# Three instead of two groups of the down product by seven products, with part of their weights narrowed earlier

## The chip, the core and the metric

The kernel runs on one core of a Trainium2 chip. The metric is the time of one execution in device microseconds (us); lower is better. The engines are TensorE (PE, matmuls; PEld is its weight load), VectorE (DVE), ScalarE (ACT), GpSimd (POOL) and SyncE (SP), which only issues DMAs here. Each engine works off its own list of instructions in order and waits on semaphores of the others.

## The reference

```python
# q, k, v: (4, 12, 448, 64)
scores = scale * np.matmul(q, k.transpose(0, 1, 3, 2))
scores = np.einsum('bhij,hg->bgij', scores, w_pre)
attn = softmax(scores)                       # over the last axis
attn = np.einsum('bhij,hg->bgij', attn, w_post)
x = np.matmul(attn, v)                       # heads put side by side: (4, 448, 768)
h = x.transpose(0, 2, 1) @ U @ V             # rank 32
u = x + h.transpose(0, 2, 1)
out = u + np.maximum(u @ w_ch1, 0.0) @ w_ch2 # 768 -> 3072 -> 768
```

An attention whose scores are mixed across the 12 heads before and after the softmax, and then a two-layer feed-forward part. The weights and U, V come as float64, so each is brought to float32 on the chip.

## The kernel before

**Stages.** The attention goes through 17 units of query rows, cut into 180 chunks; two chunks make one step. A step is a premix (matmuls with w_pre, line 502), a negated row maximum on DVE (L509), two exponents on ACT (L514), a small chain over POOL (L517), DVE (L520) and POOL (L524) that scales w_post, a postmix (56 matmuls, L538) and a copy out of PSUM (L346 on ACT, L348 on DVE). Scores (L441) are relayed by DMA on SP into a second layout (L462), and the product with v is L579 and L587. Then the rank-32 part, and from about 371 us the up product (L1056) and the down product (L1159 and L1333).

**Float32 from two parts.** For the feed-forward matmuls each operand is split into a high part and a low part, and a product is three matmuls. A split is a high half (a copy, L346 on ACT or L350 on POOL) and a low half (a subtraction, L353 on DVE or POOL), for weight tiles `w` (384 columns) and hidden tiles `u` (448 columns).

**Narrowing.** A piece of weights (128 x 384) arrives as pairs of words in a tile `kr` (DMA, L706). Five steps make float32 of it: the absolute value (L718 on ACT or L720 on DVE), then on DVE L724 with L725, L729, and L733 with L734, and a last addition L738 on POOL or DVE. The result goes to a tile `aw`, or to the single tile `ea`; from `ea` it is stored in DRAM and loaded again into `aw` when it is due (`put` and `take`: L996 and L999 for w1, L1226 and L1229 for w2). The eight pieces of the first two groups of w1 go that way during the attention.

**The down product.** w2 has 24 blocks of 128 rows. In a plain group of n rows ("S4": four rows), every batch and column block is a sum of 3n matmuls (L1159), gathered two blocks at a time by DVE (L1162); the hidden tiles are made by ACT (L1141) and DVE (L1145). In a group by seven products ("W": four rows), two batches and two column halves are computed together by seven products of mixed operands: weights are mixed at L884, hidden tiles at L1288, both on DVE or POOL, and split (L353); a block is 7 x 6 matmuls (L1333), with one copy between banks on ACT (L346) and six accumulations on DVE (L1356). Before the change four plain groups come first and two groups by seven products last; the sixteen weight pieces of the latter are narrowed through `ea` during the down product.

**What sets the order.** A planner (`Plan.order`) goes through all steps with an assumed duration for each and writes one list per engine. Ready steps are taken by rank, the smallest first; the ranks are built from the numbers in `RANK`. In the attention one unit of rank is one chunk. Steps that may run on two engines go where the planner sees the earlier end. Rings limit how far ahead it can work: 9 tiles `aw`, 21 split weight tiles, 21 split hidden tiles, 10 tiles `hs` of hidden rows, one `ea`, two `kr`, four PSUM banks of two halves.

The piece's rank and gate before the change:

```python
re = D0 + RANK["wp0"] + i * RANK["wps"]
narrow(key, src, HW, 128, re, "open_tail", partial(early_tile, key), [("ea", key)])
```

`D0` is the rank at which the down product begins, `NC` = 180 that at which the attention ends, and "open_tail" a point after the attention.

Of the kernel before, what the change touches and what calls it, by code (L numbers as in the profile page):

```python
# [34 lines left out]
HW = DM // 2  # L35
# [9 lines left out]
class Unit:  # L45
# [10 lines left out]


RANK = dict(
    e0=-99.572, estep=11.251, er=3.851, qk_lead=4.489, qk_step=0.807, av_off=3.434, av_step=1.544, post=4.6,
    kr=0.972, vr=0.941, qr=3.511, mx=1.793, ex=0.535, ep=1.385, po=3.438, qo=1.291, uv0=7.458, uvs=-0.011,  # L60
    uv1=1.407, raw=4.445, k0=-12.657, kstep=1.04, m0=8.907, pu=1.842, ev=14.526, lead=17.128, t0=-3.523,
    ts=0.611, t1=2.276, ta=38.195, tb=2.957, dl=28.391, hl=9.338, out=3, wp0=0.291, wps=18.345, wf=10.916,
    hw=8.471, hq=2.597, w1=3.04, w2=1.082, st=-3.0, un=6.124, w3=1.324,
)


GROUPS = ["S4"] * 4 + ["W"] * 2


CAPS = dict(qk=2, pre=3, post=3, av=2, lr=2, aq=2, bb=2, dn=3)  # L70
# [26 lines left out]
def words(ap):  # L97
    return ap.bitcast(I32).rearrange("p (n t) -> p n t", t=2)
# [165 lines left out]
def build(tc, q2, kt, vj, wpre_in, wpost_in, u_in, v_in, ident, w1j, w2, out, show=None):  # L264
# [64 lines left out]
    def uses(key, *at, first=False):  # L329
        for ring, k in at:  # L330
            users.setdefault((ring, k), []).append(key)
            if first:
                makers[ring, k] = key
# [57 lines left out]
    NC = len(chunks)  # L391
# [73 lines left out]
    for u, un in enumerate(units):  # L465
        b, size = un.b, 128 * (H // 2) * un.cols
        src = q2[at:at + size].rearrange("(p h i) -> p h i", p=128, h=H // 2)
# [80 lines left out]
    for k in range(NC // 2):  # L548
        r = 2 * k
        us = sorted({chunks[2 * k][0], chunks[2 * k + 1][0]})  # L550
        pre, post, st, e, wr = ("pre", k), ("post", k), ("st", k), ("e", k), ("wr", k)
        ts = [("t", u) for u in us]
# [204 lines left out]
    def early():  # L757
        c = NC + RANK["e0"] + n_early[0] * RANK["estep"]
        n_early[0] += 1
        return ("premix", max(0, int(c) // 2)), c + RANK["er"]  # L760
# [102 lines left out]
    def when(F, p, j):  # L863
        return U0 + PU * (7 * nth[F, p] + POS[j])
# [32 lines left out]
    for p in range(2):  # L897
        b0, b1 = 2 * p, 2 * p + 1
        gates = [[None] + ["open_qk"] * 3 + ["open_t1"] * 2 + ["open_mix"], ["open_tail", "open_x1", "open_x0", "open_uv", "open_uv", "open_x2", "open_x3"]][p]
        for i in range(3):  # L900
# [13 lines left out]
            t3, t2, t4, t1 = (("T", p, j, i) for j in (1, 2, 4, 5))  # L914
# [13 lines left out]
            key = ("again", i)  # L928
# [49 lines left out]
    for F in range(NF):  # L978
        r = [when(F, 0, j) - RANK["lead"] for j in range(7)]
        pieces = ((A11, 0, 0, 0), (A21, 1, 0, 1), (A22, 1, 1, 2), (A12, 0, 1, 3))  # L980
        gate = "open_qk" if F == 0 else "open_tail"
        done = {}
        for i, f, h, j in pieces:
            key = ("w", F, i)
            src = words(w1j[2 * F + f][:, h * HW:(h + 1) * HW])
# [4 lines left out]
            g, re = early()  # L990
# [84 lines left out]
    for n, (F, p) in enumerate(chains):  # L1075
# [8 lines left out]
        ev = [when(F, p, j) - RANK["ev"] for j in range(7)]  # L1084
# [13 lines left out]
    D0 = U0 + PU * 7 * NU  # L1098
    after("open_end", open_end, [("P", NU - 1, j) for j in range(7)])

    groups, base, f0, t = [], [], 0, D0
    for kind in GROUPS:
        n = 4 if kind == "W" else int(kind[1:])
# [7 lines left out]
    def take_up(ring, n=1):  # L1111
        at = [(ring, count[ring] + i) for i in range(n)]
        count[ring] += n
        return at
# [15 lines left out]
    def aw_at(k):  # L1130
        return lambda: at[pick(*k)]
# [85 lines left out]
    def early_piece(key, src, r):  # L1217
        i = pieces_w[0]
        pieces_w[0] += 1
        re = D0 + RANK["wp0"] + i * RANK["wps"]  # L1220
        narrow(key, src, HW, 128, re, "open_tail", partial(early_tile, key), [("ea", key)])
        kd = take_up("aw")[0]

        def put(eng):
            T["nf", key] = dram.tile([128, HW], F32, "nf" + "_".join(str(k) for k in key))
            eng.dma_start(out=T["nf", key], in_=T["na", key])  # L1226

        def take(eng):
            eng.dma_start(out=aw_at(kd)(), in_=T["nf", key])  # L1229

        plan.add((key, "put"), [("SP", (480, 900))], put, re, [(key, 4)], [("ea", key)])
        plan.add((key, "take"), [("SP", (480, 900))], take, r - RANK["raw"], [(key, "put")])
        uses((key, "take"), kd, first=True)
        return kd, (key, "take")
# [213 lines left out]
```

## Time and profile before

| | us |
|---|---|
| median of 3 runs | 1030.43 (1028.73 to 1030.83) |
| profiled execution | 1032.64 |
| its span, first to last instruction | 1030.8 |
| PE busy in the span | 987.8 (96%) |
| DVE busy | 787.6 (76%) |
| ACT busy | 501.1 (49%) |
| POOL busy | 362.9 (35%) |

The profile is of one execution. Busy shares are means over stages with different limits, so what a change is worth is read from its own stage. Matmuls are pipelined: a single one of 448 columns is listed with 363 ns, and its pace is read from how many end in a stretch. The idle time in front of an instruction is put down to what came last before it.

### The profile page before, as it was taken

Reading aid. Unit: us, or ns where it says so; the run is one execution under the profiler, and the core shown is the slowest. Engines: PE = TensorE matmul, PEld = TensorE weight load, DVE = VectorE, ACT = ScalarE, POOL = GpSimd, SP = SyncE. Lnnn points to the kernel's source line nnn. Section 1 sums busy time; section 2 is a strip of 40 time slices with the busy share of each in tenths; the row PEclk is TensorE's granted clock in tenths of the full one; section 3 lists DMA queues with packets and bytes.
Section 4 is the critical chain, followed back from the end, with each engine's and each line's share of the span. In section 5 each row is a group of like instructions: output and inputs, shape, how many; then the busy total and the mean of one; then the engine's idle time right before and its main releaser. Section 6 shows DMA issues by size and latency. Waiting matters only on the chain. (4 is left out here: it accounts for less than half of the span.)

```text
span 1030.8 us, 29018 instructions
## 1 busy us (share of the span) xinstructions
PE 987.8 (96%) x11964; PEld 826.7 (80%) x11964; DVE 787.6 (76%) x1303; ACT 501.1 (49%) x1038; POOL 362.9 (35%) x469
## 2 busy tenths in 40 slices
PE   7889998999989899999999999999999999999998
PEld 2556665665656589899999999999999999998987
DVE  3375764676566868989998878894899999879985
ACT  4576776767867864543333333341232332435440
POOL 4021121213111554343523434220223236647670
PEclk9999999999999999999999999999999999999999
DMA  6665657576566536445455444687354553344143
GB/s 206 203 184 170 208 173 206 160 250 174 180 205 198 160 138 217 145 139 176 153 162 148 133 137 146 201 277 299 105 176 144 175 161 115 116 139 122 49 153 115
DMA packets 96267, 173.13 MB, mean 168 GB/s; under 512 B 11576, under 2 KB 77064, under 8 KB 96136
## 3 DMA queue, kind: packets, MB, share of 16 engines
q1 hardware_dynamic: 95716, 170.64, 52.7%
q8 instruction: 94, 1.54, 0.7%
q10 hardware_dynamic: 420, 0.65, 0.2%
q14 instruction: 37, 0.30, 0.1%
HBM read 92.04 MB, written 40.50 MB: 129 GB/s over the span
## 5 line engine op out<-in xcount | busy, mean ns | idle before, releaser
L1056 PE MATMUL bank<-u,w 128*128 128x448 f32 x1512 | 305.9, 363 | 2.3 <-DVE hs L1069 1.7
L1056 PEld LDWEIGHTS bank<-u,w 128*128 128x128 f32 x1512 | 283.7, 188 | 22.6 <-DVE hs L1069 1.6
L1159 PE MATMUL bank<-u,w 128*128 128x448 f32 x1152 | 230.7, 362 | 0.0
L1159 PEld LDWEIGHTS bank<-u,w 128*128 128x128 f32 x1152 | 216.0, 188 | 14.4
L738 POOL TENSOR_TENSOR aw<-aw,x 128x384 f32<-128x384 f32 x69 | 77.2, 1120 | 187.6 <-DVE x L734 184.0
L538 PEld LDWEIGHTS bank<-wr,e 60*64 60x64 f32 x5040 | 90.7, 135 | 46.9 <-issue 29.1
L509 DVE TENSOR_REDUCE st<-bank 128x2 f32<-128x896 f32 x90 | 96.8, 1085 | 40.4 <-PE bank L502 38.9
L514 ACT ACTIVATE e<-bank,st 128x448 f32<-128x448 f32 x180 | 112.7, 638 | 21.5 <-DVE st L509 13.9
L346 ACT CAST w<-aw 128x384 fp32r<-128x384 f32 x111 | 56.2, 514 | 129.8 <-POOL aw L738 49.7
L538 PE MATMUL bank<-wr,e 60*64 60x60 f32 x5040 | 94.9, 220 | 15.5 <-issue 7.7
L1333 PE MATMUL bank<-u,w 128*128 128x448 f32 x504 | 102.6, 363 | 3.6 <-ACT bank L346 2.5
L1333 PEld LDWEIGHTS bank<-u,w 128*128 128x128 f32 x504 | 94.0, 188 | 11.9 <-ACT bank L346 3.6
L441 PE MATMUL bank<-k,q 64*64 64x448 f32 (+1 forms) x768 | 92.4, 559 | 5.7 <-DMA k<-in_kt 1.9
L517 POOL TENSOR_SCALAR st<-st 128x2 f32<-128x2 f32 x90 | 19.9, 221 | 210.1 <-ACT e L514 204.5
L502 PE MATMUL bank<-t,wpre 64*64 64x448 f32 x720 | 86.3, 550 | 6.7 <-ACT e L514 2.4
L346 ACT COPY hs<-bank 128x448 f32<-128x448 f32 x90 | 47.8, 533 | 73.4 <-PE bank L1056 69.5
L346 ACT COPY a<-bank 128x840 f32<-128x840 f32 (+1 forms) x73 | 62.1, 853 | 37.4 <-PE bank L538 36.0
L353 POOL TENSOR_TENSOR w<-aw,w 128x384 fp32r<-128x384 f32 x59 | 67.2, 1142 | 35.2 <-ACT w L346 34.5
L579 PEld LDWEIGHTS bank<-a,v 128*64 128x64 f32 x1224 | 56.6, 137 | 21.6 <-ACT a L346 6.0
L1162 DVE TENSOR_TENSOR acc<-acc,bank 128x896 f32<-128x896 f32 x48 | 51.8, 1083 | 26.3 <-PE bank L1159 26.2
L734 DVE SCALAR_TENSOR_TENSOR x<-kr,x 128x384 f32<-128x384 uint32 (+2 forms) x99 | 64.8, 655 | 3.4
L579 PE MATMUL bank<-a,v 128*64 128x120 f32 (+4 forms) x1224 | 63.5, 258 | 4.0 <-ACT a L346 2.2
(81 smaller groups left out, 1267.7 us busy)
## 6 DMA issues: line engine op xcount, KB each, us to landing
hd<-hs SPq DMA_DIRECT2D x96, 224.0 KB
hs<-hd SPq DMA_DIRECT2D x96, 224.0 KB
t<-s SPq DMA_DIRECT2D x102, 210.0 KB
kr<-in_w1j SPq DMA_DIRECT2D x48, 384.0 KB
kr<-in_w SPq DMA_DIRECT2D x48, 384.0 KB
v<-in_vj SPq DMA_DIRECT2D x24, 256.0 KB
q<-in_q SPq DMA_DIRECT2D x30, 186.0 KB
ud<-acc SPq DMA_DIRECT2D x12, 448.0 KB
```

The costliest lines, as they stand in the source:

```text
L346: eng.copy(out=o, in_=i)
L353: eng.tensor_tensor(out=o, in0=a, in1=b, op=ALU.subtract)
L441: eng.matmul(o[at, i, :S], lhsT=q[d, pj, of], rhs=k[d, pj, :], start=True, stop=True)
L502: eng.matmul(o[64 * j:64 * j + 64, i, :S], lhsT=wpre[64 * i:min(64 * i + 64, QW)], rhs=tt[side(u)][64 * i:min(64 * i + 64, QW), n, :], sta ...
L509: eng.tensor_reduce(out=mx, in_=T["pre", k][:, :, :S], axis=AX.X, op=ALU.max, negate=True)
L514: eng.activation(out=e[:, i], in_=T["pre", k][:, i, :S], func=ACTF.Exp, bias=T["mx", k][:, i:i + 1], accum_out=sm[:, i:i + 1])
L538: eng.matmul(d, lhsT=e[64 * j:64 * j + HALF, i, x * KB:x * KB + KB], rhs=wr[64 * j:64 * j + HALF, i].rearrange("p (g m) -> p g m", m=MH), ...
L579: eng.matmul(main[i * D:(i + 1) * D, c, :n], lhsT=v[:, p + c, i, x, :], rhs=a[:, x * H + 2 * (p + c) + i, :n], start=(c == 0 and x == 0), ...
L738: eng.tensor_tensor(out=f32(a), in0=f32(a), in1=f32(x), op=ALU.add)
L1056: eng.matmul(o, lhsT=w[:, x, i * 128:(i + 1) * 128], rhs=u[:, i, y, :], start=j < 2 and i + t == 0, stop=i + t == 4, skip_group_check=True)
L1159: eng.matmul(ps[:, j, :S], lhsT=wd_tile(wk[i0][f])[:, x, cc * 128:(cc + 1) * 128], rhs=h_tile(hk[f])[:, y, :], start=(i == 0), stop=(i == ...
L1333: eng.matmul(o, lhsT=wd_tile(wk[j, F])[:, x, i * 128:(i + 1) * 128], rhs=h_tile(hk[j, F])[:, y, :], start=j < 2 and t == 0, stop=t == len( ...
```

## The change

The groups become three plain and three by seven products. The first fourteen of now twenty-four weight pieces of the latter are ranked into the attention, one each 9.6 chunks from chunk 30 on, each gated by a premix; the other ten stay in the down product. The planner's numbers are set anew, among them the step of the eight w1 pieces (from 11.3 to 13.0 chunks). Nothing else is changed, so the order of all engines differs in many places.

```diff
 RANK = dict(
-    e0=-99.572, estep=11.251, er=3.851, qk_lead=4.489, qk_step=0.807, av_off=3.434, av_step=1.544, post=4.6,
...
+    e0=-99.572, estep=13.022, er=3.667, qk_lead=4.144, qk_step=0.788, av_off=4.502, av_step=1.544, post=4.6,
...
+    hw=11.881, hq=2.597, w1=4.321, w2=1.082, st=-3.0, un=5.826, w3=1.281, we=-150, ws=9.631,
 )
-GROUPS = ["S4"] * 4 + ["W"] * 2
+GROUPS = ["S4"] * 3 + ["W"] * 3
+
+
+AHEAD = 14
@@
     def early_piece(key, src, r):
         i = pieces_w[0]
         pieces_w[0] += 1
-        re = D0 + RANK["wp0"] + i * RANK["wps"]
-        narrow(key, src, HW, 128, re, "open_tail", partial(early_tile, key), [("ea", key)])
+        re, gate = D0 + RANK["wp0"] + max(0, i - AHEAD) * RANK["wps"], "open_tail"
+        if i < AHEAD:
+            c = NC + RANK["we"] + i * RANK["ws"]
+            re, gate = c + RANK["er"], ("premix", min(max(0, int(c) // 2), NC // 2 - 1))
+        narrow(key, src, HW, 128, re, gate, partial(early_tile, key), [("ea", key)])
```

Line numbers up to the function above grow by 3, those behind it by 6. In the rows that follow, a tile's number tells one buffer from another.

DVE in the attention, between two row maxima some 32 steps in, before and after (`st` the row maxima and sums, `a` and `s` the copies out of PSUM, `t` and `u` parts of the rank-32 part and of the up product's operand):

```order
L348 COPY a_321<-bank_60 128x42x20
L520 RECIPROCAL st_271<-st_271 128x2
L509 TENSOR_REDUCE st_252<-bank_58 128x2
L520 RECIPROCAL st_433<-st_433 128x2
L353 TENSOR_TENSOR u<-acc,u 128x448
L520 RECIPROCAL st_252<-st_252 128x2
L601 TENSOR_TENSOR acc<-acc,bank_60 128x3x11x5
L509 TENSOR_REDUCE st_259<-bank_59 128x2
```

```order
L723 TENSOR_SCALAR x_791<-kr_690 128x384
L356 TENSOR_TENSOR t_0_1907<-bank_59,t_0_1907 32x256
L727 TENSOR_SCALAR x_791<-x_791 128x384
L728 TENSOR_SCALAR ea_790<-x_791 128x384
L732 SCALAR_TENSOR_TENSOR ea_790<-kr_690,ea_790 128x384
L833 TENSOR_TENSOR acc<-acc,bank_60 128x2x448
L736 TENSOR_SCALAR x_791<-ea_790 128x384
L737 SCALAR_TENSOR_TENSOR x_791<-kr_690,x_791 128x384
L512 TENSOR_REDUCE st_433<-bank_59 128x2
```

A whole narrowing (L723 to L737) now stands in front of a row maximum there.

PE at the end of the attention, before and after (`wr`, `e`: postmix; `a`, `v`: the product with v; `u`, `w`: the up product):

```order
L538 MATMUL bank_60<-wr_282,e_261 64x12x5 x24
L538 MATMUL bank_60<-wr_282,e_261 64x60 x4
L538 MATMUL bank_59<-wr_319,e_274 64x12x5 x24
L538 MATMUL bank_59<-wr_319,e_274 64x60 x4
L538 MATMUL bank_61<-wr_354,e_285 64x12x5 x24
L538 MATMUL bank_61<-wr_354,e_285 64x60 x4
L1045 MATMUL bank_58<-u,w_5539 128x448 x2
L1056 MATMUL bank_60<-u,w_5539 128x448 x9
L579 MATMUL bank_59<-a_321,v_267 64x100 x18
```

```order
L541 MATMUL bank_61<-wr_282,e_261 64x12x5 x24
L541 MATMUL bank_61<-wr_282,e_261 64x60 x4
L1048 MATMUL bank_60<-u,w_5644 128x448 x2
L1059 MATMUL bank_59<-u,w_5644 128x448 x9
L541 MATMUL bank_61<-wr_319,e_274 64x12x5 x24
L541 MATMUL bank_61<-wr_319,e_274 64x60 x4
L1059 MATMUL bank_59<-u,w_5645 128x448 x9
L541 MATMUL bank_58<-wr_354,e_285 64x12x5 x24
L541 MATMUL bank_58<-wr_354,e_285 64x60 x4
L582 MATMUL bank_61<-a_321,v_267 64x100 x18
```

Two products of the up product (L1059) moved between the last three postmixes.

DVE in the blocks by seven products, in the second group of each, before and after (`acc<-bank,acc`: accumulations; `u<-hs,u`: low halves of hidden tiles; `hs<-hs,hs`: mixings of hidden tiles; `ea`, `x`: narrowing):

```order
L1356 TENSOR_TENSOR acc<-bank_59,acc 128x448
L724 TENSOR_SCALAR x_930<-x_930 128x384
L725 TENSOR_SCALAR ea_790<-x_930 128x384
L353 TENSOR_TENSOR u<-hs_5956,u 128x448
L729 SCALAR_TENSOR_TENSOR ea_790<-kr_824,ea_790 128x384
L1356 TENSOR_TENSOR acc<-bank_58,acc 128x448 x2
L1356 TENSOR_TENSOR acc<-bank_59,acc 128x448
L733 TENSOR_SCALAR x_930<-ea_790 128x384
L734 SCALAR_TENSOR_TENSOR x_930<-kr_824,x_930 128x384
```

```order
L1294 TENSOR_TENSOR hs_6090<-hs_6090,hs_6088 128x448
L1362 TENSOR_TENSOR acc<-bank_59,acc 128x448 x2
L1362 TENSOR_TENSOR acc<-bank_60,acc 128x448
L356 TENSOR_TENSOR u<-hs_6090,u 128x448
L1294 TENSOR_TENSOR hs_6094<-hs_6089,hs_6091 128x448
L1362 TENSOR_TENSOR acc<-bank_61,acc 128x448
L1362 TENSOR_TENSOR acc<-bank_60,acc 128x448
L356 TENSOR_TENSOR u<-hs_6094,u 128x448
L1362 TENSOR_TENSOR acc<-bank_58,acc 128x448
L356 TENSOR_TENSOR u<-hs_6087,u 128x448
```

The narrowing is gone from this place, and mixings and low halves stand between the accumulations.

## Rows read from the trace of the kernel before

**Rows 1.** Windows by stage: stretch, busy us of each engine (instructions), clock, DMA.
```profile
57.70:360.80 303.10, 284.11 (x7310) 188.33 (x7304) 196.58 (x332) 222.50 (x483) 70.66 (x184) 0.99 0.61 189
...
690.00:920.50 230.50, 230.50 (x1154) 216.12 (x1153) 197.59 (x306) 68.56 (x131) 86.21 (x78) 1.00 0.50 161
920.50:1027.90 107.40, 103.06 (x508) 94.40 (x507) 88.06 (x129) 46.16 (x92) 58.19 (x48) 1.00 0.37 119
```

**Rows 2.** A window inside the sums, and the sums' matmuls: ns min/median/max, first and last.
```profile
700.00:750.00 50.00, 50.00 (x252) 46.88 (x251) 32.83 (x51) 10.78 (x21) 7.79 (x8) 1.00 0.55 196
...
L1159 PE MATMUL bank<-u,w x1152: 360/363/364, 688.1 to 920.1; 128*128 128x448 f32 x192
```

**Rows 3.** Timeline of PE in the blocks: start, us, instruction [idle before <-what ended it].
```profile
951.08 15.88 PE L1333 MATMUL bank<-u,w 128*128 128x448 f32 x78 [1.86 <-ACT bank L346]
967.36 27.95 PE L1333 MATMUL bank<-u,w 128*128 128x448 f32 x138 [0.39 <-DVE acc L1356]
```

**Rows 4.** Window from the first to the 55th accumulation, columns as in rows 1.
```profile
923.90:1001.20 77.30, 74.38 (x367) 68.24 (x367) 68.76 (x99) 41.53 (x83) 52.74 (x44) 1.00 0.37 114
```

**Rows 5.** DVE's groups by form in that window: count | busy, mean ns | idle before.
```profile
L1356 DVE TENSOR_TENSOR acc<-bank,acc 128x448 f32<-128x448 f32 x52 | 30.8, 616 | 9.1 <-PE bank L1333 5.9 <-ACT bank L346 3.0
L353 DVE TENSOR_TENSOR u<-hs,u 128x448 fp32r<-128x448 f32 x16 | 17.0, 1072 | 0.0
L1288 DVE TENSOR_TENSOR hs<-hs,hs 128x448 f32<-128x448 f32 x11 | 10.3, 957 | 0.0
L729 DVE SCALAR_TENSOR_TENSOR ea<-kr,ea 128x384 int32<-128x384 int32 x3 | 2.9, 967 | 0.0
...
L353 DVE TENSOR_TENSOR w<-aw,w 128x384 fp32r<-128x384 f32 x3 | 2.1, 694 | 0.0
L884 DVE TENSOR_TENSOR aw<-aw,aw 128x384 f32<-128x384 f32 x2 | 2.0, 990 | 0.0
...
L733 DVE TENSOR_SCALAR x<-ea 128x384 int32<-128x384 int32 x3 | 1.5, 506 | 0.0
```

**Rows 6.** DVE's narrowing and copies by form from 170 to 350 us.
```profile
L348 DVE COPY s<-bank 124x896 f32<-124x896 f32 x10 | 10.9, 1086 | 5.8 <-PE bank L441 5.0 <-issue 0.4 <-ACT e L514 0.2
...
L734 DVE SCALAR_TENSOR_TENSOR x<-kr,x 128x384 f32<-128x384 uint32 x8 | 4.7, 582 | 0.3
L729 DVE SCALAR_TENSOR_TENSOR ea<-kr,ea 128x384 int32<-128x384 int32 x8 | 4.4, 550 | 0.1
...
L725 DVE TENSOR_SCALAR ea<-x 128x384 int32<-128x384 int32 x8 | 3.0, 381 | 0.3
L724 DVE TENSOR_SCALAR x<-x 128x384 f32<-128x384 f32 x8 | 2.9, 362 | 0.1
L733 DVE TENSOR_SCALAR x<-ea 128x384 int32<-128x384 int32 x8 | 2.8, 352 | 0.1
L720 DVE TENSOR_SCALAR x<-kr 128x384 int32<-128x384 int32 x7 | 2.5, 358 | 3.6 <-DMA kr<-in_w1j 3.6
```

**Rows 7.** Three gaps of PE in the attention, from its timeline.
```profile
178.40 0.37 PE L538 MATMUL bank<-wr,e 60*64 60x60 f32 x3 [2.65 <-issue]
...
251.90 0.98 PE L502 MATMUL bank<-t,wpre 64*64 64x448 f32 x8 [0.99 <-DVE acc L601]
...
298.16 1.62 PE L579 MATMUL bank<-a,v 128*64 128x90 f32 x36 [1.47 <-ACT e L514]
```

**Rows 8.** The last postmix on PE.
```profile
369.15 1.45 PE L538 MATMUL bank<-wr,e 60*64 60x60 f32 x56 [1.84 <-ACT a L346]
```

**Rows 9.** DVE's low half of a hidden tile alone, and beside an instruction of POOL.
```profile
954.34 0.61 DVE L353 TENSOR_TENSOR u<-hs,u 128x448 fp32r<-128x448 f32 x1
...
960.98 1.16 POOL L353 TENSOR_TENSOR u<-hs,u 128x448 fp32r<-128x448 f32 x1 [3.80 <-ACT u L346]
...
963.19 1.27 POOL L1288 TENSOR_TENSOR hs<-hs,hs 128x448 f32<-128x448 f32 x1
...
963.37 1.57 DVE L353 TENSOR_TENSOR u<-hs,u 128x448 fp32r<-128x448 f32 x1
```

More of the change, by code (lines that the diff above doesn't have):

```diff
@@ L58 @@
 RANK = dict(
-    e0=-99.572, estep=11.251, er=3.851, qk_lead=4.489, qk_step=0.807, av_off=3.434, av_step=1.544, post=4.6,
[L60 to L63, printed above, removed]
-)
-GROUPS = ["S4"] * 4 + ["W"] * 2
+    e0=-99.572, estep=13.022, er=3.667, qk_lead=4.144, qk_step=0.788, av_off=4.502, av_step=1.544, post=4.6,
+    kr=0.972, vr=0.969, qr=3.511, mx=1.793, ex=0.535, ep=1.385, po=2.659, qo=1.291, uv0=7.458, uvs=0.277,
+    uv1=1.407, raw=3.874, k0=-11.774, kstep=1.03, m0=9.512, pu=1.661, ev=14.526, lead=17.128, t0=-3.523,
+    ts=1.27, t1=2.44, ta=38.195, tb=2.957, dl=31.544, hl=9.338, out=2.962, wp0=0.291, wps=17.853, wf=8.982,
+    hw=11.881, hq=2.597, w1=4.321, w2=1.082, st=-3.0, un=5.826, w3=1.281, we=-150, ws=9.631,
+)
+GROUPS = ["S4"] * 3 + ["W"] * 3
+AHEAD = 14
 CAPS = dict(qk=2, pre=3, post=3, av=2, lr=2, aq=2, bb=2, dn=3)
```

## The prediction

> **What bounds the kernel now.** I read the stretches first, then the gaps of TensorE (PE), then what the other engines do around them. From 690 us on, the down product runs: PE is busy 230.50 of 230.50 us in the plain sums, and 103.06 of 107.4 us in the two groups by seven products [rows 1]. In the sums 252 matmuls take 50.00 us [rows 2], so a matmul of 448 columns costs 0.1984 us and PE knows no wait there. VectorE (DVE) is nearly as full: 197.59 of 230.5 us in the sums and 88.06 of 107.4 us in the blocks [rows 1]. The attention is different: from 57.7 to 360.8 us PE has 284.11 us of work in 303.1 us, DVE 196.58, ScalarE (ACT) 222.50, GpSimd (POOL) 70.66 [rows 1]. There PE waits for short chains, and room is left on DVE. So fewer matmuls shorten the end one for one, as long as DVE and POOL can feed PE in the blocks and the attention does not pay for what is moved into it.
>
> **Part 1: one plain group becomes a group by seven products.** A plain group of four rows of w2 has 4 batches x 6 blocks x 4 rows x 3 = 288 matmuls; by seven products it has 2 x 3 x 7 x 6 = 252. That is 36 fewer, 36 x 0.1984 = **-7.1 us**, all of it on the path, since in the sums nothing but PE ends a wait [rows 1, 2]. No other engine can take this away without PE showing gaps, so the rest of the prediction is about gaps.
>
> **Part 2: the blocks need more of DVE and POOL.** Each column block takes six accumulations on DVE, and half a group (three blocks, 126 matmuls, 25.0 us of PE) takes 18. In the profile the first three halves run from 923.9 us to 1001.2 us, 77.3 us where PE alone would need 75.0: a stall of 2.3 us, with gaps of 1.86 and 0.39 us [rows 3]. DVE is busy 68.76 us of it, 22.9 us a half, and idle 2.85 us a half [rows 4]. The instructions of that stretch add up to 73.3 us: five rows in full, and five rows of narrowing, of which the largest (2.9 us) and the smallest (1.5 us) are shown, that add up to 11.1 [rows 5]; that is 0.94 us of busy time for each us in that sum.
>
> Now the same for the new order. DVE has, from the first accumulation to the 91st, that is five halves: 90 accumulations, 41 low halves of hidden tiles, 24 mixings of hidden tiles, 4 low halves and 2 mixings of weights, and one narrowing where three stood in three halves. At the means of [rows 5], with 3.7 us for the narrowing (11.1 / 3), that is 55.4 + 44.0 + 23.0 + 2.8 + 2.0 + 3.7 = 130.9 us, x 0.94 = 122.8 us, 24.6 us a half. PE needs 25.0. DVE goes from 92% to 98% of PE's time. The extra is not narrowing; it is low halves of hidden tiles, which now must be made for the next group while one runs, with no light last group until later.
>
> What that costs depends on how much DVE still idles. The bounds: 0.4 us a half, so that it just keeps up (25.0 us), and the 2.85 us of [rows 4] unchanged (27.45 us). Much of the idle time of today is DVE waiting for a product of PE (5.9 of the 9.1 us in the accumulations' row [rows 5]), and that wait shrinks when DVE is the later one. I take the middle, 1.6 us: 26.2 us a half, a stall of 5 x 1.2 = 6.0 us in place of 2.3, **+3.7 us** (bounds -2.3 and +9.9). The last half has little beside its accumulations in both orders, and I leave it alone.
>
> **Part 3: fourteen narrowings go into the attention.** By the order of instructions, DVE has 22 narrowings before the last row maximum, where it had 11 (three of the eight w1 pieces moved later in turn, since their step grew). One costs DVE 0.362 + 0.381 + 0.550 + 0.352 + 0.582 = 2.23 us, and 0.358 us more where DVE takes the absolute value [rows 6], nine more of them. So 11 x 2.23 + 9 x 0.36 = 27.8 us are added. The new order also gives 12 of DVE's 56 copies out of PSUM to ACT, at about 1.0 us (1.086 us for the larger form [rows 6]): net +16 us of DVE in a stretch with over 100 us of room. ACT takes 12 more copies, some 11 us on 222.50 of 303.1 us [rows 1]; I price that at nothing, because ACT still has 70 us of slack, and at some tenths of a us a copy if the slack is not where the copies are.
>
> What does DVE work cost PE there? The eight w1 pieces of today put 8 x (2.23 + 0.36) = 20.7 us on DVE between 170 and 350 us. Of the gaps of PE in that time, two follow from a DVE instruction that came late: 0.99 us at 251.90, ended by an addition on DVE, just after a piece whose first instruction waited for its raw load, and 1.47 us at 298.16, behind such a piece too (two such waits, 3.6 us of DVE [rows 6]) [rows 7]. The gap of 2.65 us at 178.40 [rows 7] opens before the first piece's first instruction, in the middle of a postmix, and is not theirs. So 2.46 us per 20.7 us, 0.12 us of PE per us of DVE: 16 x 0.12 = **+1.9 us**. Below: nothing, if each piece sits in idle time of DVE. Above: all three gaps laid to the pieces, 5.1 / 8 = 0.64 us a piece, 11 pieces, +7.0 us.
>
> SP is moved past too: 14 raw loads and 14 stores of narrowed pieces now stand among the relays of the scores, and eight stores and eight loads of narrowed pieces are new altogether. A store waits for POOL's last step and holds the relays behind it. Today's eight stores sit in the same place and no gap of PE in [rows 7] ends on a relay, so I price this inside the +1.9 us.
>
> **Part 4: the seam.** At the end of the attention the old order runs three postmixes in a row; the last waits 1.84 us for ACT to empty a bank [rows 8]. The new order puts the first two up-products (9 matmuls each, 1.8 us) between them. I credit most of that gap: **-1.5 us** (bounds 0 and -1.84). In return three narrowings now fall right behind the last row maximum; until the fourth of the first up-chains' additions the new order has 7 low halves of u on DVE there where the old has 17, and I call that even.
>
> **The sum.** -7.1 + 3.7 + 1.9 - 1.5 = -3.0 us. The profiled execution took 1032.64 us with a span of 1030.8 us, so 1.8 us lie around the span and do not change; by its own time the changed kernel takes 1029.6 us. The profiled run lies 2.2 us above the median of 1030.43 us, so against the median the forecast is **1027.4 us**.
>
> **Rival 1: DVE and POOL become the bound of the blocks.** If the idle time of DVE stays at 2.85 us a half, the five halves take 137.2 us and the tail gains -7.1 + 9.9 = +2.8 us; with the attention's +0.4 that is 1033.6 us. For it: DVE is at 98% of PE's time by count, and its queue is in order, so one instruction that stands holds up the accumulations behind it and these hold the banks. One such case shows now: at 963.37 a low half on DVE takes 1.57 us beside a POOL instruction that began at 963.19, where the same form at 954.34 took 0.61 us [rows 9], and PE's gap at 967.36 follows [rows 3]. Against it: the narrowings that stood in that queue are gone but one. It decides from 26.9 us a half: there the tail's loss is 7.1 us more than today's 2.3. I give it a fifth, since some of the blocks' work is done ahead, in the sums.
>
> The Trainium skill, SBUF — State Buffer, section Who interferes with whom, says that a DVE instruction with two SBUF inputs and a GpSimd instruction that reads SBUF share one port pair by an exclusive lock: whichever starts second blocks for the whole of the other. The trace agrees: 1.57 us is 0.61 us of work behind POOL's 1.27 us. By that rule the pair has 95 DVE instructions of at most 0.61 us and 83 POOL ones of at most 1.16 us in the three groups, 154 us beside PE's 150 (an estimate from this kernel's counts and the rows). A stall of 4 us would then be a floor, and the sum no better than -7.1 + 1.7 + 0.4 = -5.0 us, 1025.4 us; it speaks against rival 3 and leaves the forecast.
>
> **Rival 2: the attention pays.** With 0.64 us a piece, +7.0 instead of +1.9, the sum is +2.1 us, 1032.5 us. The place would be the chains from row maximum over exponent to postmix, which wait behind DVE's narrowing and, on SP, behind stores that wait for it. Slower than before from an attention that costs 4.9 us before the seam's credit.
>
> **Rival 3: all of it is covered.** DVE keeps up (stall as today, 2.3 us) and the attention costs nothing: -7.1 - 1.5 = -8.6 us, 1021.8 us. Speaking for it: 100 us of room in the attention.
>
> **Rival 4: the pieces come late.** The first block group waits for its taken pieces, and the saving goes there: about no change. Against it: they are stored 300 us and more ahead.
>
> **How the numbers follow.** A difference under 0.2% (2.1 us) can hardly be told from none here. Forecast 0.50, its own range 1025.0 to 1029.5: 0.33 faster, 0.17 same. Rival 1 0.20: 0.14 slower, 0.06 same. Rival 2 0.14: 0.09 slower, 0.05 same. Rival 3 0.13, faster. Rival 4 0.03, same. Together faster 0.46, same 0.31, slower 0.23. The range goes from rival 3 to rival 1: 1022.0 to 1034.0 us, which leaves about a tenth out on each side.
>
> **What would show it.** Step 1: matmuls of the sums at 0.1984 us and 36 fewer. Step 2: the spacing of the 1st, 19th, 37th accumulation and so on, 26.2 us a half, against 25.8 today; 27 us and more is rival 1. Step 3: the start of the first matmul of the sums, 688.1 us today [rows 2], with the same work of PE ahead of it in both: within 2 us of that; a start 5 us later is rival 2, 1.5 us earlier rival 3. Step 4: no gap over 1 us among the last three postmixes. Wrong would be the whole frame if PE showed gaps in the up product or the sums, which have next to none today.

## The result, and the profile after

The changed kernel is **slower**: 1040.74 us median of 5 runs (1036.28 to 1043.48) against 1029.18 us for the kernel before. The ratio on record over the runs is 1.0096 with a 95% interval of 1.0073 to 1.0120; the two medians by themselves give 1.0112. The forecast was 1027.4 us with a range up to 1034. The profiled execution took 1040.88 us with a span of 1038.5 us. In the code of after, the lines up to the early pieces stand 3 lower than before, those behind them 6 lower.

The trace falls into two parts that went opposite ways. The first view is the windows by stage, with the columns of [rows 1]: attention (from the same row maximum to the last one), sums, blocks.

```profile
57.80:381.40 323.60, 292.81 (x7513) 191.51 (x7506) 215.05 (x390) 235.30 (x507) 84.78 (x196) 0.99 0.66 202
...
706.30:881.70 175.40, 175.40 (x879) 164.40 (x878) 145.54 (x217) 52.67 (x100) 74.04 (x67) 1.00 0.51 164
881.70:1034.60 152.90, 151.57 (x757) 141.31 (x755) 127.74 (x188) 73.69 (x148) 99.31 (x82) 1.00 0.33 107
```

The attention's window is 20.5 us longer than that of [rows 1] (323.6 against 303.1 us). From its end to the start of the sums the changed kernel takes 324.9 us, the kernel before 327.3 us, so the whole loss lies in the attention. The second view is the lines of the matmuls of the sums and of the blocks (ns of one, first and last start):

```profile
L1162 PE MATMUL bank<-u,w x864: 360/362/363, 706.3 to 881.5; 128*128 128x448 f32 x173
```
```profile
L1339 PE MATMUL bank<-u,w x756: 360/362/477, 881.7 to 1034.6; 128*128 128x448 f32 x189
```

The sums begin at 706.3 us, where [rows 2] had 688.1: **18.2 us lost ahead of them**. From there to the end of the span it takes 332.2 us, against 342.7 before: **10.5 us won behind them**. I call these two the front and the tail. The tail is the same in the five traces of after's order to within 0.4 us, so a median less the tail of its profile gives the median front: 708.5 us after, 686.5 before, 22.0 us apart, and this is what the table below compares. (The profiled run of before was 1.5 to 3.5 us over its medians, after's was at its own; so the trace shows the smaller loss.)

How the tail was won stands in the chain of work that ended last (start, us, what) and in DVE's groups over the first five halves:

```profile
900.46 132.29 PE bank L1339 x660
```
```profile
884.83:1007.58 122.75, 122.13 (x611) 114.07 (x610) 109.72 (x162) 69.69 (x141) 91.66 (x76) 1.00 0.31 98
```
```profile
L1362 DVE TENSOR_TENSOR acc<-bank,acc 128x448 f32<-128x448 f32 x89 | 52.7, 617 | 11.9 <-ACT bank L349 7.3 <-PE bank L1339 4.0
L356 DVE TENSOR_TENSOR u<-hs,u 128x448 fp32r<-128x448 f32 x40 | 36.1, 913 | 1.1 <-ACT u L349 0.7
L1294 DVE TENSOR_TENSOR hs<-hs,hs 128x448 f32<-128x448 f32 x24 | 21.3, 899 | 0.0
```

660 matmuls run in one unbroken piece of the chain. The first and the 91st accumulation (884.83 and 1007.58 us) are apart by five halves of 24.55 us, PE's own pace of 25.0 us a half or a little less. DVE idles 13 of the 122.75 us. Where [rows 3] show PE waiting 1.86 us for ACT, after has no such gap.

The front is harder to read, for the loss has no one place. These are four of the larger gaps on PE, three in the attention and one in the up product (timeline: start, us, instruction, [idle before <-what ended it]); such rows don't add up to 18 us, and each has another releaser:

```profile
260.41 0.98 PE L505 MATMUL bank<-t,wpre 64*64 64x448 f32 x8 [1.95 <-ACT e L517]
...
312.60 0.98 PE L505 MATMUL bank<-t,wpre 64*64 64x448 f32 x8 [3.12 <-issue]
...
348.47 1.04 PE L541 MATMUL bank<-wr,e 60*64 60x60 f32 x56 [1.53 <-POOL wr L527]
...
403.92 2.08 PE L1059 MATMUL bank<-u,w 128*128 128x448 f32 x9 [2.66 <-DVE xl L356]
```

Up to the sums PE idles 48.3 us where it idled 35.8. That is 12.5 of the 18.2 us; the other 5.7 us are busy time of PE, 658.0 us against 652.4, for the same matmuls. The seam itself is as forecast, the last three postmixes with no gap ahead of them:

```profile
383.38 0.99 PE L541 MATMUL bank<-wr,e 60*64 60x60 f32 x56
...
387.17 1.04 PE L541 MATMUL bank<-wr,e 60*64 60x60 f32 x56
...
390.16 1.04 PE L541 MATMUL bank<-wr,e 60*64 60x60 f32 x56
```

### The profile page after: what moved, and what is told of

It reads as the page before. It is cut to its first block, busy times and chain, and to the rows that moved or that the text cites. A ratio compares the mean times of both kernels' runs of the same rounds, so it can differ in the third digit from the quotient of the medians.

```text
span 1038.5 us, 29068 instructions
## 1 busy us (share of the span) xinstructions
PE 985.3 (95%) x11928; PEld 819.3 (79%) x11928; DVE 798.1 (77%) x1323; ACT 525.9 (51%) x1082; POOL 417.4 (40%) x511
## 5 line engine op out<-in xcount | busy, mean ns | idle before, releaser
L1059 PE MATMUL bank<-u,w 128*128 128x448 f32 x1512 | 305.3, 362 | 3.4 <-DVE xl L356 2.7
L1059 PEld LDWEIGHTS bank<-u,w 128*128 128x128 f32 x1512 | 282.8, 187 | 23.7 <-DVE xl L356 3.0
L1162 PE MATMUL bank<-u,w 128*128 128x448 f32 x864 | 173.3, 362 | 0.0
L1162 PEld LDWEIGHTS bank<-u,w 128*128 128x128 f32 x864 | 162.0, 187 | 10.8
L1339 PE MATMUL bank<-u,w 128*128 128x448 f32 x756 | 151.9, 362 | 1.3 <-DVE acc L1362 1.3
L1339 PEld LDWEIGHTS bank<-u,w 128*128 128x128 f32 x756 | 141.5, 187 | 11.6 <-DVE acc L1362 2.1
L741 POOL TENSOR_TENSOR aw<-aw,x 128x384 f32<-128x384 f32 x64 | 72.5, 1133 | 146.9 <-DVE x L737 146.9
L541 PEld LDWEIGHTS bank<-wr,e 60*64 60x64 f32 x5040 | 88.5, 135 | 52.5 <-issue 30.1
L349 ACT CAST w<-aw 128x384 fp32r<-128x384 f32 x117 | 59.8, 515 | 105.3 <-DVE aw L887 28.8
L520 POOL TENSOR_SCALAR st<-st 128x2 f32<-128x2 f32 x90 | 21.3, 237 | 208.4 <-ACT e L517 207.1
L356 POOL TENSOR_TENSOR w<-aw,w 128x384 fp32r<-128x384 f32 x66 | 75.1, 1143 | 31.4 <-ACT w L349 25.6
L1362 DVE TENSOR_TENSOR acc<-bank,acc 128x448 f32<-128x448 f32 x108 | 64.3, 618 | 24.3 <-PE bank L1339 12.5
L349 ACT COPY a<-bank 128x840 f32<-128x840 f32 (+1 forms) x76 | 65.2, 859 | 34.9 <-PE bank L541 33.6
L349 ACT CAST u<-hs 128x448 fp32r<-128x448 f32 x85 | 46.7, 567 | 48.4 <-DVE hs L1294 23.9
```

The source lines that it names most:

```text
L349: eng.copy(out=o, in_=i)
L356: eng.tensor_tensor(out=o, in0=a, in1=b, op=ALU.subtract)
L541: eng.matmul(d, lhsT=e[64 * j:64 * j + HALF, i, x * KB:x * KB + KB], rhs=wr[64 * j:64 * j + HALF, i].rearrange("p (g m) -> p g m", m=MH), ...
L741: eng.tensor_tensor(out=f32(a), in0=f32(a), in1=f32(x), op=ALU.add)
L1059: eng.matmul(o, lhsT=w[:, x, i * 128:(i + 1) * 128], rhs=u[:, i, y, :], start=j < 2 and i + t == 0, stop=i + t == 4, skip_group_check=True)
L1162: eng.matmul(ps[:, j, :S], lhsT=wd_tile(wk[i0][f])[:, x, cc * 128:(cc + 1) * 128], rhs=h_tile(hk[f])[:, y, :], start=(i == 0), stop=(i == ...
```

## The experiments

All runs in one table; the front in the trace is the start of the sums, the median front is the median less the tail, and the last column sets it against 686.5 us.

| run | median us | ratio to before [95%] | front in the trace | tail | median front | against before |
|---|---|---|---|---|---|---|
| before | 1029.18 | | 688.1 | 342.7 | 686.5 | |
| after | 1040.74 | 1.0096 [1.0073, 1.0120] | 706.3 | 332.2 | 708.5 | +22.0 |
| e_ranks | 1064.49 | 1.0336 [1.0293, 1.0379] | 695.3 | 365.2 | 699.3 | +12.8 |
| e_groups | 1085.09 | 1.0541 [1.0493, 1.0589] | 688.0 | 400.3 | 684.8 | -1.7 |
| e_ahead | 1070.95 | 1.0399 [1.0347, 1.0450] | 730.8 | 340.5 | 730.5 | +44.0 |
| e_groups_ahead | 1063.51 | 1.0311 [1.0262, 1.0361] | 729.4 | 334.8 | 728.7 | +42.2 |
| t_all | 1033.54 | 1.0047 [1.0024, 1.0071] | 693.7 | 332.2 | 701.3 | +14.8 |
| t_comp | 1037.07 | 1.0076 [1.0047, 1.0106] | 705.8 | 332.2 | 704.9 | +18.4 |
| t_dma | 1036.43 | 1.0083 [1.0053, 1.0114] | 698.3 | 332.6 | 703.8 | +17.3 |
| t_step4 | 1040.13 | 1.0117 [1.0072, 1.0163] | 703.1 | 332.5 | 707.6 | +21.1 |
| o_all | 1043.99 | 1.0123 [1.0058, 1.0188] | 707.6 | 334.8 | 709.2 | +22.7 |
| f_idle | 1067.15 | 1.0350 [1.0297, 1.0403] | 731.4 | 333.5 | 733.7 | +47.2 |
| f_due | 1045.99 | 1.0158 [1.0109, 1.0208] | 712.7 | 333.5 | 712.5 | +26.0 |
| h14 | 1031.76 | 1.0011 [0.9984, 1.0038] | 699.8 | 332.2 | 699.6 | +13.1 |
| h12 | 1032.45 | 1.0023 [1.0007, 1.0039] | 694.4 | 336.2 | 696.3 | +9.8 |
| h10 | 1037.61 | 1.0070 [1.0046, 1.0094] | 695.3 | 343.7 | 693.9 | +7.4 |
| h14_all | 1019.48 | 0.9887 [0.9854, 0.9920] | 688.5 | 332.2 | 687.3 | +0.8 |
| h14b | 1028.61 | 0.9991 [0.9958, 1.0025] | 692.6 | 332.2 | 696.4 | +9.9 |
| h12b | 1030.64 | 1.0005 [0.9982, 1.0027] | 691.1 | 336.5 | 694.1 | +7.6 |

The median of before moved between 1029.18 and 1031.16 us over these groups of runs, and single executions of one kernel lie up to 15 us apart (h14b: 1023.05 to 1037.94), so a median front is good to some 2 us at best, and a front in one trace to less: those of t_all and t_dma are of their fastest executions. For e_ranks and e_groups no second trace shows that the tail stays the same; there the median front is an estimate.

### Which part of the change costs: one part at a time

The change has three parts: other ranks, three groups by seven products, fourteen early pieces. e_ranks has the new ranks alone, e_groups the new groups alone, e_ahead the early pieces alone, e_groups_ahead groups and pieces.

```
 GROUPS = ["S4"] * 3 + ["W"] * 3      # e_groups, e_groups_ahead; the others ["S4"] * 4 + ["W"] * 2
 AHEAD = 14                           # e_ahead, e_groups_ahead; the others 0
 RANK = dict(e0=-99.572, estep=13.022, ...)   # e_ranks: of after; the others: of before
```

> The new numbers of RANK alone: four plain groups and two by seven products as before, no piece narrowed in the attention. In the changed kernel the sums begin at 706.3 us, in the kernel before at 688.1 us. Theory N (the 14 narrowings cost the attention its time): sums begin at 686 to 692 us, time within 4 us of before. Theory R (the new ranks made a worse order for the attention, whatever is narrowed there): sums begin at 700 us or later, time 1038 us or more.

> The groups alone: three plain and three by seven products, old ranks, all 24 pieces narrowed in the down product. Both theories: sums begin at 688 us, as before. Then -7.1 us of PE against 8 more narrowings of 2.2 to 2.6 us on DVE in the down product; the time is 1022 us if DVE takes them in, and up to 1040 us if the blocks wait for pieces that rank late.

> The early pieces alone: old ranks, four plain groups and two by seven products, 14 of their 16 pieces narrowed in the attention. Theory N: sums begin at 700 us or later, tail a few us shorter than before (its stall of 6.7 us in the blocks goes), time 1036 to 1042 us. Theory R: sums begin at 688 to 693 us, time 1024 to 1030 us.

> The whole change with the old ranks: three groups by seven products, 14 pieces narrowed in the attention. Theory N: sums begin at 700 us or later, then some 332 us as in the changed kernel, time 1036 to 1042 us. Theory R: sums begin at 688 to 693 us, time 1020 to 1027 us, better than both kernels.

None of the expectations fits as it stands. e_ranks, at 695.3 us, lies between the bounds of theory N and theory R; e_ahead and e_groups_ahead begin the sums late, as N had it, but at 1071 and 1064 us they are far slower than its 1036 to 1042 us; and e_groups was expected between 1022 and 1040 us and took 1085.

The groups alone leave the front where it was and ruin the tail. The windows of e_groups, 100 us out of its blocks, columns as in [rows 1], show PE busy 58.61 us beside DVE's 85.51:

```profile
913.00:1013.00 100.00, 58.61 (x266) 52.17 (x264) 85.51 (x150) 34.75 (x67) 40.90 (x35) 0.82 0.35 108
```

So early narrowing is what lets the blocks keep pace; it takes 65.5 us off the tail (400.3 to 334.8). But under the old ranks it puts 42 to 44 us on the front. Under the new ranks it puts on only 9 more than those ranks cost alone, 22.0 against 12.8 (by the trace of e_ranks 8.8 in place of 12.8: 695.3 against 686.5 us). So the new ranks make room for the pieces, and that room costs some 9 to 13 us before a single piece stands in it (and a tail of 365.2 us, where none is narrowed early).

### How much is the work of the pieces?

Here every instruction of after keeps its place in its queue, and the fourteen pieces shrink. t_all: engine steps on 8 of 384 columns, raw loads and stores of one column; t_comp: the engine steps only; t_dma: the transfers only; t_step4: POOL's last step only. o_all shrinks all in the order of e_groups_ahead. What is left out is that much of the narrowing of these pieces. (t_comp and t_dma also set the tiles that would hold old values to zero once, at the start.)

```
         def load_raw(eng):
-            eng.dma_start(out=T["raw", key], in_=src)
+            c = 1 if small else n
+            eng.dma_start(out=T["raw", key][:, :c], in_=src[:, :c])
...
-            return T["raw", key], T["nx", key][:p, :n], T["na", key].bitcast(I32)[:p, :n]
+            c = m if small else n
+            return T["raw", key][:, :c], T["nx", key][:p, :c], T["na", key].bitcast(I32)[:p, :c]
```

> The changed kernel in its own order, with all that the 14 early pieces do in the attention shrunk: their steps work on 8 columns instead of 384, their raw load and their store on one, so their values are left out; every instruction stays in its place. Theory T (the time of the narrowing's instructions, on DVE and POOL, and of their transfers): the sums begin within 4 us of the kernel before, at 686 to 692 us, time some 1022 to 1027 us. Theory O (the order of all other work was made worse to let them in): the sums still begin at 700 us or later, time 1036 us or more.

> As the run before, but only the steps on ACT, DVE and POOL are shrunk to 8 columns; raw loads and stores stay whole. If the engines' time is what costs (theory T, engines): sums begin at 686 to 694 us. If the transfers and SP's queue cost (theory T, transfers): 700 us or later. Theory O: 700 us or later.

> The counterpart: raw loads and stores of the 14 pieces are shrunk to one column, the steps on the engines stay whole (on zeros that were set ahead). Engines: sums begin at 702 to 708 us, as in the changed kernel. Transfers: 686 to 695 us. Theory O: 700 us or later.

> Only the last step of the 14 pieces (the addition on POOL, about 1.0 us) is shrunk to 8 columns. If it is POOL that makes the scaling in the softmax chain late: sums begin 5 us or more earlier than 706 us. If DVE: within 3 us of 706 us.

> The old ranks with three groups by seven products and fourteen narrowings early (sums began at 729.4 us there, 41 us later than before), with the order of all instructions kept, but each step of the fourteen pieces on 8 columns and their raw loads and stores on one column; so nearly none of their work is done. Theory D: the order keeps most of the loss, the sums begin at 712 us or later. Theory Q: most of the loss goes with the work, the sums begin before 700 us.

Of the 22.0 us, 7.2 go with the work (1040.74 to 1033.54 us). The medians of the parts are 3.7 us lower without the engine steps, 4.3 without the transfers and 0.6 without POOL's step, but the intervals of all three overlap that of after, so none of them can be told from nothing; that of t_all (up to 1.0071) just clears it (from 1.0073). **14.8 us stay with next to no work left in the pieces**: that is the order in which all the other work now stands, with whatever the emptied steps still hold up where they stand. Under the old ranks it is 19.5 and 22.7 us. The expectations had asked for a plainer answer: t_all's 1033.54 us lies between theory T (to 1027) and theory O (from 1036), and the 707.6 us of o_all between theory Q (before 700) and theory D (from 712).

### Holding the old order

If the order is at fault, the old order with the pieces put in between should be cheap. f_idle and f_due hold every queue in before's order up to the sums (2600 steps, HELD lists step and engine); f_idle lets a piece's step go only where the planner has nothing else ready on that engine, f_due where it is due (without the last two lines of the diff). The step of the w1 pieces is set back to 11.251 in both, as in all held runs below.

```
+    for e in ("SP", "PE", "ACT", "DVE", "POOL"):
+        plan.lines.append([k for k, x in HELD if x == e])
+    for k, e in HELD:
+        engines, *rest = plan.steps[k]
+        plan.steps[k] = ([(o, c) for o, c in engines if o == e], *rest)
...
...
+        if i < AHEAD:
+            re += 1e4
```

> The changed kernel, but every other instruction up to the sums stands in its queue exactly in the order of the kernel before, on the engine it had there; the fourteen narrowings, in full, are put between them only where the plan's clock sees an engine with nothing else ready. The blocks and their ranks are as in the changed kernel. Theory D (it is the displaced order of all the other work that costs, the fourteen pieces themselves cost the 7 us that shrinking them gave back): the sums begin at 690 to 697 us, the tail takes 332 to 336 us, 1026 to 1035 us in all. Theory Q (the pieces hold up in-order queues wherever they stand, and the plan's new order only made room for them): the sums begin at 705 us or later, 1040 us or more.

> As the run before, but a narrowing that is due goes first where it and other work are both ready, in place of last. Theory D: within 3 us of the run before. Theory Q: the sums begin some 3 to 10 us later than in the run before, since the pieces stand ahead of the chains from row maximum to postmix more often.

My theory D fell: 47.2 and 26.0 us, more than in the changed kernel. Theory Q had the size of f_idle, but f_due begins the sums 18.7 us earlier than f_idle, where Q wanted it 3 to 10 us later. The traces of these two show what costs in them. Waits of DVE in the attention of f_due, and then of f_idle (us in total, times, longest):

```profile
DVE ea L835 <- DMA nfv<-ea: 13.8, 5, 5.2
```
```profile
DVE ea L835 <- DMA nfv<-ea: 27.6, 6, 10.7
```

ea is the one tile that every finished piece passes through. In the timeline of f_due a piece follows on the heels of another:

```profile
309.74 1.07 POOL L848 TENSOR_TENSOR ea<-ea,x 128x384 f32<-128x384 f32 x1 [1.88 <-DVE x L844]
...
310.84 0.34 SPq L1339 DMA_DIRECT2D nfv<-ea  x1
...
316.20 0.36 DVE L835 TENSOR_SCALAR ea<-x 128x384 int32<-128x384 int32 x1 [5.17 <-DMA nfv<-ea]
316.47 0.29 DVE L711 TENSOR_TENSOR acc<-acc,bank 128x135 f32<-128x135 f32 x1
...
316.82 1.31 PE L903 MATMUL bank<-ident,acc 128*112 128x128 f32 x5 [5.71 <-DVE acc L711]
```

The store is issued at 310.84 us, right behind POOL's last step of its piece, and lets the next writer go 5.4 us later. The next piece's step stands at the head of DVE's queue all that time; an addition (L711) waits behind it, and PE stands still for 5.71 us until that is done. In f_idle the longest wait has a second part. POOL's last step ended at 261.41 us, but SP issued the store only at 272.57 us, behind fourteen other transfers of its own list:

```profile
260.41 1.00 POOL L848 TENSOR_TENSOR ea<-ea,x 128x384 f32<-128x384 f32 x1 [1.87 <-DVE x L844]
...
272.57 0.36 SPq L1341 DMA_DIRECT2D nfv<-ea  x1
...
278.47 0.36 DVE L835 TENSOR_SCALAR ea<-x 128x384 int32<-128x384 int32 x1 [10.75 <-DMA nfv<-ea]
```

This is what costs in the two held orders and not what costs in the changed kernel, where DVE waits 0.2 us in all for such a store.

### Searched places

So the same order and the same work with other places. A search moved the seven steps of each piece, and those of the eight w1 pieces that share the tile, among the other steps, which stay as in before; it minimised the end of the front in a model of the five in-order queues with the planner's own costs and an assumed time on top for a raw load and a store to land. The search could also give a step the other of its two engines. h14, h12 and h10 have fourteen, twelve and ten pieces early; h14b and h12b have none before 45 us; h14_all is h14 with the pieces on 8 columns. The edit is the list HELD of the runs above, and the gates of these pieces are gone, since the list sets their places:

```
-        plan.add((key, 0), [("SP", (480, 1800 * s))], load_raw, rank - RANK["raw"], [gate], [raw])
+        plan.add((key, 0), [("SP", (480, 1800 * s))], load_raw, rank - RANK["raw"], [gate] * bool(gate), [raw])
...
-            re, gate = c + RANK["er"], ("premix", min(max(0, int(c) // 2), NC // 2 - 1))
+            re, gate = c + RANK["er"], None
```

> Before's order of every other instruction up to the sums, as in the two runs with the held order, but the seven steps of each of the fourteen pieces (and of the eight w1 pieces that share their tiles) are placed by a search over places, so that none stands at the head of a queue while the one tile for finished pieces is not yet stored, or a raw load not yet landed. Theory places (what costs is where the steps stand: VectorE's queue held by a store that has not landed): the sums begin at 693 to 700 us, against 712.7 with the places by due time; the tail 333 to 336 us. Theory amount (each piece costs its share wherever it stands, the 24.6 us of the held order divided by fourteen): 706 us or later.

> As the run with fourteen searched places, but twelve pieces in the attention and two more late. Theory places: the sums begin at 690 to 696 us, the tail 0 to 4 us longer than with fourteen. Theory amount: 704 us or later.

> As the run with fourteen searched places, but ten pieces in the attention and four more late. Theory places: the sums begin at 688 to 692 us, nearly free; the tail 0 to 10 us longer than with fourteen; if it is under 4 us this is faster than both kernels, about 1026 us. Theory amount: 702 us or later.

> The run with fourteen searched places, order and places unchanged, but the steps of the fourteen pieces work on 8 columns each and their raw loads and stores move 8 columns, so their work is left out almost wholly (the sums began at 699.8 us with it). Theory rest-is-work (what the search could not hide is the pieces' own time on the engines and the memory): the sums begin at 687 to 691 us. Theory rest-is-places (instructions of the pieces at queue heads hold others, whatever they last): 695 us or later.

> As the run with fourteen searched places, but no piece before 45 us, where raw loads stood ahead of the first q and k loads (the first row maximum came at 23.2 us there, 20.5 in the kernel before). If that start is a loss carried to the end: the sums begin at 696 to 699 us, about 1029 us in all. If the places lost there come back as waits later: 700 to 704 us.

> As the run with twelve searched places (sums at 694.4 us, tail 336.2 us), but no piece before 45 us. If the start is a loss carried to the end: the sums begin at 691 to 694 us, about 1027 to 1030 us in all, which would be a hair under the kernel before; otherwise 696 us or later.

The starts of the sums in f_due, h14, h14b and h14_all, each the line of their matmuls in its trace:

```profile
L1269 PE MATMUL bank<-u,w x864: 360/362/363, 712.7 to 887.9; 128*128 128x448 f32 x173
```
```profile
L1274 PE MATMUL bank<-u,w x864: 360/362/364, 699.8 to 875.0; 128*128 128x448 f32 x173
```
```profile
L1274 PE MATMUL bank<-u,w x864: 360/362/363, 692.6 to 867.8; 128*128 128x448 f32 x173
```
```profile
L1280 PE MATMUL bank<-u,w x864: 360/362/363, 688.5 to 863.7; 128*128 128x448 f32 x173
```

From 712.7 to 692.6 us (in the medians from 712.5 to 696.4) with the same work in other places, a few of its steps on another engine: up to the sums, nine of the 23 last additions of whole pieces run on DVE in h14b, where f_due has all of its 24 on POOL. DVE's wait to write the next piece until a store has landed is no longer among its waits. Which of the two, places or engines, won how much no run tells. In the attention of h14b PE works 287.91 of 307.7 us, with as much work on DVE as in f_due (228.11 us here, 228.24 there from 57.2 to 386.5 us):

```profile
57.20:364.90 307.70, 287.91 (x7372) 189.10 (x7366) 228.11 (x409) 227.09 (x495) 79.55 (x189) 1.00 0.68 212
```

With the work out, the held order starts the sums at 688.5 us, before's time to 0.4 us (0.8 in the medians): in the places of h14 the steps as such cost nothing, and the 12.3 us that h14 pays over h14_all are the pieces' work. h14b pays 9.1 us over the same base. Against t_all, which has the emptied pieces in the changed kernel's order and a median front of 701.3 us, h14_all is 14.0 us better: with next to no narrowing in either, that is the price of the order and of the places. The start matters little more than the medians scatter: h14b is 3.2 us below h14, its trace 7.2. Fewer early pieces win 3 to 6 us in front and lose 4.0 (twelve) or 11.5 us (ten) in the tail, where DVE must narrow beside the accumulations. So h14, h12 and h14_all came out as theory places and theory rest-is-work had it; h10 did not (695.3 us for at most 692, a tail 11.5 us longer for at most 10). The traces of h14b (692.6 us) and h12b (691.1) begin the sums as early as expected or earlier, but h12b's 1030.64 us misses its 1027 to 1030.

No version beats both kernels by more than can be measured. h14b is some 12 us faster than the changed kernel and equal to the kernel before (0.9991 [0.9958, 1.0025]); h14_all, at 1019.48 us, shows what the change would bring if the narrowing were free.

## Why the prediction was wrong

**Part 1, right.** 36 matmuls fewer, each at the 0.1984 us of [rows 2], and nothing in the sums took that back (PE 175.40 of 175.40 us).

**Part 2, wrong in sign.** Forecast 26.2 us a half and +3.7 us; measured 24.55 us, and the tail fell by 3.4 us beyond Part 1's 7.1. The counts held (40 low halves where 41 were forecast, 24 mixings). The mis-sized term is DVE's own time. It was busy 109.72 us for the five halves, 21.9 us a half, not 24.6: the low halves took 36.1 us in place of 44.0, since one took 913 ns where I carried over 1072 from [rows 5] (why they are shorter, no run shows); the mixings 21.3 us in place of 23.0; and the instructions of that stretch add up to some 120 us, 0.91 us of busy time for each, not 0.94. The accumulations' 52.7 us in place of 55.4 are mostly my counting: I took ninety at their mean length, while the busy column of [rows 5], 30.8 us for 52, makes that 53.3 us. DVE's idle time stayed, 2.6 us a half against 2.85 [rows 4], just as rival 1 had it; with 21.9 us of work it did no harm. The blocks took 153.3 us for 150.0 us of matmuls, a stall of 3.3 us. Counted likewise, the two groups of before took 106.9 us (920.33 to 1027.20) for 508 matmuls, 100.8 us: a stall of 6.1 us, of which the forecast counted the 2.3 us of three halves, so most of the 3.4 us is stall that fell. By the rule of the Trainium skill (SBUF — State Buffer, Who interferes with whom) I had estimated a floor of 4 us of stall. The measured 3.3 us lies under it, and since that estimate took each instruction at its longest, it was no floor; the waits that the profile shows for PE there come to 1.3 us, and no run here tells a port from a queue.

**Part 3, the step that failed.** Forecast +1.9 us, with bounds 0 and 7.0; step 3 wanted the sums within 2 us of 688.1. The front lost 18.2 us in the trace, 22.0 in the medians. Two errors are in it. The price per piece was taken near its lower end, 0.12 us of PE for each us of DVE. With everything else held in its old order and the pieces well placed, they cost 9.1 us, 0.65 us a piece for fourteen. That this is rival 2's price (0.64) is luck: that price took in a gap which I had myself put down to no piece. In the changed kernel's own order 7.2 us go with the work. Transfers may have a share, which t_dma can't tell from nothing, and I had priced SP inside the 1.9 us. The larger error is what the sum left out: I priced the pieces as if all else stayed as it was, while the order showed otherwise. The ranks were set anew and the whole attention was put in another order; 14.8 us of the 22.0 stay when the pieces do next to nothing, and some 9 to 13 us come with the new ranks and no piece at all. One part of this was in the prediction, the copies that go from DVE to ACT, and I priced it at nothing. PE's waits that ACT ended, added up to the sums, were 13.7 us before, 18.8 after and still 18.5 in t_all, but 9.8 in h14_all; f_due, with the copies where they were, has 16.5, and no run gave the copies back alone, so it is a hint and not a share that is shown. No row of the kernel before could price the new order, so the bound above should have been far wider than 7.0 us.

**Rival 2** had the right sign and stage, and its sentence on chains behind DVE and behind stores is what f_due shows; in the changed kernel itself DVE does not stand waiting for such a store, and its 1032.5 us fell 8 us short. Rivals 1 and 4 did not come: the tail is shorter than rival 3 had it, and the waits that the profile shows for PE in the blocks are for accumulations and not for taken pieces.

**Part 4, right.** The last postmix has no gap; but a gap of 2.66 us now stands among the first up products (L1059 at 403.92); the largest there before was 1.25 us (L1056 at 414.19).

**What stays open.** Which instructions of the displaced order cost the 14.8 us: the gaps are small, many and have different releasers, and no run undid a part of that order. What part of the 12.3 us in h14 is DVE's time and what the transfers': the 3.7 us of t_comp and the 4.3 us of t_dma are within the scatter.

## What to carry to other kernels

When a change re-sets the numbers by which a planner orders work, price the re-ordering first: run the new order with the added work shrunk to nothing, and the new numbers without the addition; here some two thirds of the loss stayed without the work. Work that is put into idle time of an in-order queue is cheap only if nothing it waits for can be late: with one tile for all pieces, look for the store that has to be issued and to land before the next piece may write, and leave that time between them. Idle time of an engine is no price list: the same extra VectorE time in the attention, some 31 us, cost 9.9 us or 26.0 us by its places and by the engine of a few steps.

## What the runs showed of the hardware

A store of 192 KB out of SBUF, issued at 310.84 us, let the next writer of its tile go at 316.20 us (f_due): 5.4 us, of which DVE stood 5.17. In f_idle it was 5.9 us (272.57 to 278.47), with 11.2 us before it in which the store waited for its turn on SP.

A long gap of PE cost more than its own length. In f_idle PE waited 11.5 us for a row maximum behind such a store (281.32), and the window around it shows a granted clock of 0.62: 0.50, TensorE's lower level of 1.2 GHz, from 276 to 284 us, and 1.00 again from 286 us. In the window ahead, in which the gap began, it was 0.96:

```profile
264.00:276.00 12.00, 5.58 (x168) 2.62 (x164) 1.64 (x6) 2.87 (x6) 1.38 (x4) 0.96 0.91 261
276.00:288.00 12.00, 6.68 (x132) 4.68 (x136) 7.12 (x15) 5.23 (x14) 2.38 (x6) 0.62 0.20 68
```
```profile
281.32 1.77 PE L612 MATMUL bank<-t,wpre 64*64 64x448 f32 x8 [11.50 <-DVE st L619]
```

That group of eight took 1.77 us there, where the same group took 0.98 us at 260.41 in after. Up to the sums PE was busy 663.6 us in f_idle, 658.0 in after and 652.4 in before, for the same work. The starved blocks of e_groups show the same, a clock of 0.82 with PE busy 58.61 of 100 us.
